# The last third of an MLP weight held behind another unit's keys, and a new hand-written order for the first batch

## The chip, the cores and the metric

The kernel runs on one core of one Trainium2 chip. The core has TensorE (PE; its weight loads are shown apart as PEld), VectorE (DVE), ScalarE (ACT), GpSimd (POOL) and SyncE (SP), which run side by side and wait for each other by semaphores. Each takes its own instructions in the order in which the program lists them. Transfers between HBM and on-chip memory are issued from the queues of SP, ACT and POOL and run on 16 shared DMA engines. The metric is device time in microseconds, the median of several executions; lower is better.

## The reference

Inputs are q, k and v of shape (8, 12, 448, 64): batches, heads, tokens, head width.

```python
def rmsnorm(x, g):
    rms = np.sqrt(np.mean(x * x, axis=-1, keepdims=True) + 1e-06)
    return x / rms * g
q_n, k_n = (rmsnorm(q, g_q), rmsnorm(k, g_k))
scores = scale * np.matmul(q_n, k_n.transpose(0, 1, 3, 2))
attn = softmax(scores)                                  # over the keys
x = np.matmul(attn, v) -> transposed to (8, 448, 768)
xn = (x - mean) / np.sqrt(var + 1e-06) * g_ln
out = x + np.maximum(xn @ w_ch1, 0.0) @ w_ch2           # 768 -> 3072 -> 768
```

## The kernel before

**Tiling.** Heads go in pairs: a batch has 6 pairs, and pair p = 6 * batch + number. The inputs come in units. Units 0 to 3 are the first batch; from unit 4 on a unit is two pairs (four heads), so batch 1 is units 4 to 6, batch 2 units 7 to 9, and unit 4 holds pairs 6 and 7, unit 5 pairs 8 and 9, unit 6 pairs 10 and 11. The keys, queries and values of a unit are each loaded by one DMA of 384 KB (tokens 0 to 383, `load_main`, line 169) and two of 32 KB (the 64 tokens left, `load_left`, line 177), from the SP queue for all units of the first 118 us but one DMA. Unit tiles from unit 5 on use two buffers in turn, so unit u + 2 can be loaded only when all readers of unit u are through.

**Weights.** The two MLP matrices are read in five pieces from GpSimd's queue: W0, W1 and W2 are the thirds of the first weight (`load_w1`, line 961, 1536 KB each as stored), W3 and W4 the halves of the second (`load_w2`, line 966, 2304 KB each). A piece that stands in `BEHIND` first copies two elements of a unit's tile into a scratch tile, `poke` (line 837), and so waits until that unit's load has landed; the number behind the unit is 0 for queries, 1 for keys, 2 for values. All that GpSimd has after it in the list waits too.

```python
BEHIND = {0: (4, 1), 2: (5, 2), 3: (6, 2), 4: (7, 2)}
def weights(c):
    if c in BEHIND:
        u, n = BEHIND[c]
        g = 6 * UNITS[u][2]
        nc.gpsimd.tensor_copy(out=poke, in_=self.loads[u][n][:, g - 1:g + 1, 0])
    if c < 3:
        self.load_w1(1024 * c, 1024 * c + 1024)
    else:
        self.load_w2(c - 3)
```

**Order.** The order of all instructions of the first stage is written out by hand in `ORDER`, a list of 580 short names; `first_attention` calls what each stands for, one after the other, on all five engines (tc.manual_schedule). The first stage covers the first batch's attention, layer norm and the up half of its MLP, the attention of the second batch, and most of the first batch's down half. Later work (`run_rest`) is laid out by a rule and is not touched. The names, with the engine that does each:

- `F12`: 12 filler matmuls of 128 columns on TensorE (line 877), whose result nobody reads.
- `L6k`, `L6q`, `L6v`: loads of a unit's keys, queries, values (SP). `W0` to `W4`: the weight pieces (POOL). `G` loads the norm's gains, `G2` scales them (POOL, line 885).
- For a unit u from 4 on: `a`, `c` square keys and queries, `d`, `e` sum the squares (DVE, line 265), `g` takes the inverse roots (ACT), `i` multiplies the keys by the gains (POOL, line 273), `j` makes their 16-bit copy, `k` the rest that this copy leaves (DVE, line 281), `l` scales the queries (DVE, line 93), `m` doubles them (line 318), `v`, `za`, `zb` copy the values (POOL, lines 321 and 327).
- For the first batch, in parts: `a`, `d`, `h`, `n`, `j`, `k` for the keys; `qa`, `qG` (times gains, line 604), `qt`, `ql` (scaled, line 611), `qm` (doubled, line 617), `Q0.0` to `Q2.4` (turned on TensorE) and `QC` (moved out of PSUM) for the queries; `z`, `za`, `zb` for the values (POOL, lines 660 and 665).
- `K8`, `Q8`: keys and queries of pair 8 turned on TensorE (lines 341 to 344, 358 to 361); all such turns write one PSUM tile, `tr`, which `C8`, `D8` empty (DVE, lines 351 and 366).
- `S`, `E`, `V`, `O`: scores (TensorE), their powers (ACT), times values (TensorE), divided by the sums (DVE). `T`, `A`, `N`, `X`, `XC`: layer norm and its turn. `U0.4`: a group of 24 matmuls of the up half (line 748), tile 0, columns 4 * 512 and on of the first weight, so U.0 and U.1 read W0, U.2 and U.3 W1, U.4 and U.5 W2; `R0.4` its relu. `H`, `J`, `P`: the down half (line 1088), which reads W3 for the first 384 columns and W4 for the others, its sum and its store. `Y.`: the second batch's layer norm, `Y.X` its turns by DMA.

`ENGINE` gives, for operations that several engines can do, the engine where it is not the usual one (A for ACT, V for DVE, P for POOL). Usual are ACT for `a`, `c`, `j` and `R`, POOL for `i` and `qG`, DVE for `n`, `m`, `qm`, `QC` and `C`.

Of the kernel before, what the change touches and what calls it, by code (L numbers as in the profile page):

```python
# [35 lines left out]
ORDER = """
F12 a0 d0 h0 sp1 a1 L4k G qa0.0 n0 spm sp2 L4q j0 qt0.0 d1 qG0.0 k0 F14 K0 h1 ql0.0 n1 a2 Q0.0
qa0.2 j1 C0 k1 d2 qt0.2 QC0.0 F2 K1 F10 S0.0.0 qa1.0 qG0.2 a3 qt1.0 qG1.0 d3 h2 S0.0.1 E0.0.1
E0.0.0 h3 C1 n2 n3 ql0.2 W0 j2 F36 S0.1.0 S0.1.1 k2 F9 Q0.2 K2 ql1.0 C2 W1 j3 E0.1.0 F5 Q1.0
E0.1.1 K3 QC0.2 S0.2.0 k3 z2 qa2.0 C3 S0.2.1 Q1.3 qt2.0 K4 C4 E0.2.0 E0.2.1 S0.3.0 qa2.4 z0 za2  # L40
S0.3.1 zb2 za0 QC1.0 zb0 hq E0.3.1 E0.3.0 z3 F6 K5 za3 S0.4.0 zb3 G2 S0.4.1 C5 QC1.3 V0.0
E0.4.0 qt2.4 qG2.0 E0.4.1 S0.5.0 S0.5.1 V0.1 E0.5.0 S1.0.0 V0.2 E0.5.1 L4v S1.0.1 V0.3 O0.0
E1.0.0 S1.1.0 E1.0.1 E1.1.0 V0.4 S1.1.1 E1.1.1 ql2.0 S1.2.0 S1.2.1 hr qm2.0 V0.5 V1.0 O0.1 V1.1
E1.2.1 S1.3.0 T0.1 T0.0 E1.2.0 E1.3.0 Q2.0 S1.3.1 b4 a4 V1.2 S1.4.0 qG2.4 E1.3.1 Q2.2 S1.4.1 A0
QC2.0 E1.4.0 N0 V1.3 S1.5.0 E1.4.1 S1.5.1 ql2.4 V1.4 E1.5.0 S2.0.0 O1.0 X0 E1.5.1 S2.0.1 E2.0.0
E2.0.1 V1.5 XC0 S2.0.2 L5k L5v E2.0.2 qm2.4 QC2.2 Q2.4 O1.1 d4 S2.1.0 c4 S2.1.1 U0.0 E2.1.1
E2.1.0 S2.1.2 S2.2.0 T1.1 T1.0 e4 E2.1.2 V2.0 A1 N1 S2.2.1 U0.1 E2.2.0 i4 S2.2.2 E2.2.1 j4 g4
l4 S2.3.0 m4 R0.0 E2.2.2 V2.1 S2.3.1 X1 E2.3.0 E2.3.1 QC2.4 S2.3.2 E2.3.2 XC1 V2.2 S2.4.0
E2.4.0 S2.4.1 L5q Q6 k4 D6 W2 V2.3 E2.4.1 R0.1 S2.4.2 O2.0 E2.4.2 S2.5.0 K6 E2.5.0 V2.4 S2.5.1
S2.5.2 C6 E2.5.2 T2.0 U1.0 R1.0 E2.5.1 b5 a5 c5 V2.5 O2.1 S6.0 E6.0 S6.1 K7 U1.1 S6.2 v4 E6.1  # L50
S6.3 E6.2 U1.2 E6.3 i5 za4 S6.4 T2.1 C7 A2 L6k d5 e5 v5 zb4 S6.5 U1.3 Q7 batch1 R1.1 N2 D7 j5
E6.4 L6v S6.6 k5 U0.2 E6.5 X2 R1.3 g5 l5 za5 S7.0 E6.6 V6.0 XC2 zb5 S7.1 V6.1 E7.0 L6q V6.2
V6.3 V6.4 W3 L7k V6.5 R0.2 E7.1 b6 a6 V6.6 S7.2 L7q K8 C8 O6 S7.3 m5 E7.3 E7.2 v6 i6 U0.3 L7v
za6 Q8 S7.4 V7.0 V7.1 S7.5 E7.4 E7.5 D8 V7.2 V7.3 U1.4 S7.6 S8.0 K9 d6 R1.2 c6 e6 E8.0 C9 zb6
j6 R0.3 U0.4 g6 U2.0 Q9 V7.4 k6 E7.6 V7.5 S8.1 S8.2 l6 L8k m6 R2.0 R0.4 E8.2 D9 U2.1 S8.3 V7.6
K10 b7 a7 i7 O7 U2.2 E8.3 R2.1 E8.1 S8.4 R2.2 S8.5 E8.4 L8v U2.3 V8.0 V8.1 E8.5 d7 S8.6 c7 U1.5
V8.2 j7 E8.6 R2.3 U0.5 E9.6 S9.0 C10 R0.5 V8.3 V8.4 V8.5 E9.0 S9.1 T7 V8.6 R1.4 U2.4 Q10 S9.2
e7 E9.1 O8 R1.5 k7 D10 v7 V9.0 S9.3 V9.1 E9.3 g7 l7 U2.5 Q11 S9.4 W4 E9.2 S9.5 E9.4 D11 E9.5
H0.0.0 S10.0 V9.2 za7 S10.1 E10.0 L8q K11 V9.3 b8 a8 V9.4 S10.2 V9.5 V9.6 E10.2 E10.1 H0.0.1
S10.3 m7 H0.0.2 E10.3 S10.4 S10.5 O9 R2.5 E10.4 V10.0 C11 zb7 E10.5 c8 R2.4 V10.1 V10.2 H0.0.3  # L60
Q12 v8 i8 L9k V10.3 S10.6 E10.6 H1.0.0 d8 S11.0 H1.0.1 T9 D12 j8 V10.4 e8 V10.5 E11.6 za8 V10.6
R S11.1 zb8 H1.0.2 O10 k8 E11.1 E11.0 K12 S11.2 H1.0.3 J0.0 S11.3 V11.0 g8 L9v L9q E11.2 V11.1
H2.0.0 S11.4 V11.2 E11.3 l8 C12 J1.0 S11.5 H2.0.1 E11.5 E11.4 K13 V11.3 S12.0 S12.1 m8 V11.4
V11.5 C13 V11.6 H2.0.2 E12.0 L10k O11 T11 S12.2 H2.0.3 H0.1.0 Y.A H0.1.1 E12.2 H0.1.2 Y.N2 Y.N0
S12.3 H0.1.3 x8 L10v L10q H1.1.0 Q13 E12.3 Y.X0 H1.1.1 S12.4 Y.R E12.4 J0.1 Y.N1 H1.1.2 H1.1.3
H2.1.0 S12.5 Y.X1 Y.X2 J2.0 E12.1 E12.5 H2.1.1 H2.1.2 D13 Y.N3 J1.1 Y.X3 H2.1.3 y8 J2.1 P2.1
P1.1 P0.1 P2.0 M
""".split()
# [1297 lines left out]
```

## Time and profile before

| | us |
|---|---|
| median of 3 runs | 596.11 |
| lowest and highest | 591.86, 599.5 |
| the profiled execution, its own time | 598.79 |
| its span in the profile | 597.1 |
| TensorE busy | 580.4 (97%) |
| DVE, ACT, POOL busy | 297.2, 346.6, 187.5 |
| the 94 filler matmuls, busy | 8.9 |
| last matmul group of the down half in the list (H2.1.3) begins | 117.2 |

A row of the order of time has start, duration, engine, line, operation, output <- inputs, and in brackets the engine's idle time before it with what ended it. A row of busy time by stretches has the stretch, its length, and for PE, PEld, DVE, ACT and POOL the busy time with the number of instructions, then the granted TensorE clock (1.00 is full), the DMA engines' share and the GB/s that they moved. A row of a DMA queue has packets, MB and the share of the 16 engines' time: q1 is SP's queue, q0 GpSimd's. A row of DMA issues has the transfer, the number of them, the size of one and the median time from issue to landing. A row of a group has its line and form, its number, then busy time and mean duration in ns, then idle time before it.

### The profile page before, as it was taken

Reading aid. Unit: us, or ns where it says so; the run is one execution under the profiler, and the core shown is the slowest. Engines: PE = TensorE matmul, PEld = TensorE weight load, DVE = VectorE, ACT = ScalarE, POOL = GpSimd, SP = SyncE. Lnnn points to the kernel's source line nnn. Section 1 sums busy time; section 2 is a strip of 40 time slices with the busy share of each in tenths; the row PEclk is TensorE's granted clock in tenths of the full one; section 3 lists DMA queues with packets and bytes.
Section 4 is the critical chain, followed back from the end, with each engine's and each line's share of the span. In section 5 each row is a group of like instructions: output and inputs, shape, how many; then the busy total and the mean of one; then the engine's idle time right before and its main releaser. Section 6 shows DMA issues by size and latency. Waiting matters only on the chain.

```text
span 597.1 us, 12428 instructions
## 1 busy us (share of the span) xinstructions
PE 580.4 (97%) x4974; PEld 362.5 (61%) x4974; DVE 297.2 (50%) x645; ACT 346.6 (58%) x654; POOL 187.5 (31%) x255
## 2 busy tenths in 40 slices
...
GB/s 258 211 241 218 196 211 205 148 113 144 153 142 141 105 133 137 177 135 88 153 108 115 140 105 149 192 121 126 133 56 90 86 63 1 27 106 1 1 53 56
DMA packets 130225, 75.24 MB, mean 126 GB/s; under 512 B 96469, under 2 KB 120357, under 8 KB 130165
## 3 DMA queue, kind: packets, MB, share of 16 engines
...
## 4 chain that ended last, share of the span: by engine, by line
PE 83%; DMA 7%; SPq 4%; DVE 4%; POOL 1%; issue 1%; POOLq 0%; DVEq 0%
PE psC L1088 35%; PE psH L1054 33%; PE psS L407 7%; DMA qkv<-in_v_dram 6%; PE oA L476 5%; SPq L177 2%; PE oB L478 2%; PE psS L425 1%; SPq L169 1%; DMA w<-in_k_dram 1%; DMA xnT<-xn 0%; DVE hT L758 0%; POOL v L660 0%; SPq L1036 0%; POOL vl L665 0%
## 5 line engine op out<-in xcount | busy, mean ns | idle before, releaser
L1088 PE MATMUL psC<-w,hT 128*128 128x384 f16 (+1 forms) x1368 | 235.6, 323 | 0.0
L1054 PE MATMUL psH<-xnT,w 128*128 128x512 f16 (+1 forms) x1008 | 217.3, 356 | 0.4 <-DMA xnT<-xn 0.4
L439 ACT ACTIVATE E<-psS,rr_all 128x448 f16<-128x448 f32 x264 | 164.5, 635 | 67.4 <-PE psS L407 66.8
L1088 PEld LDWEIGHTS <-hT 128*128 128x128 f16 x1368 | 128.2, 98 | 76.1 <-issue 0.4
L1056 ACT ACTIVATE hT<-psH 128x512 f16<-128x512 f32 (+1 forms) x168 | 93.7, 558 | 114.9 <-PE psH L1054 113.3
L1054 PEld LDWEIGHTS <-w 128*128 128x128 f16 x1008 | 91.1, 98 | 77.6 <-issue 2.9
L407 PE MATMUL psS<-qU,kU 128*128 128x448 f16 x252 | 86.7, 354 | 0.0
L476 PEld LDWEIGHTS <-E 128*128 128x128 f16 x792 | 53.9, 99 | 34.6 <-issue 2.5
L1095 DVE SCALAR_TENSOR_TENSOR x<-psC,rs_all,x 128x384 f32<-128x384 f32 x48 | 29.1, 616 | 77.9 <-PE psC L1088 77.4
L273 POOL TENSOR_TENSOR qkv<-qkv,gprod 128x896 f32<-128x896 f32 x19 | 39.5, 2079 | 76.6 <-ACT khl L118 62.1
L476 PE MATMUL oA<-v,E 128*128 128x65 f16 x756 | 57.8, 194 | 0.1
L489 DVE RECIPROCAL rec_all<-oA 128x6 f32<-128x6 f32 x42 | 8.2, 195 | 88.0 <-PE oA L476 87.7
L265 DVE TENSOR_REDUCE ssq<-khl 128x14 f32<-128x896 f32 x21 | 22.7, 1081 | 53.6 <-ACT khl L118 53.6
L169 POOL DMA_DIRECT2D qkv<-in_k_dram x14 | 11.1, 796 | 118.3 <-ACT E L439 53.4
L478 PE MATMUL oB<-v,E 128*128 128x65 f16 x252 | 45.1, 194 | 0.1
L407 PEld LDWEIGHTS <-kU 128*128 128x128 f16 x252 | 24.3, 98 | 15.2
L265 DVE TENSOR_REDUCE ssq<-qn 128x14 f32<-128x896 f32 x21 | 22.8, 1084 | 20.9 <-ACT qn L118 20.9
L93 DVE SCALAR_TENSOR_TENSOR qn<-qkv,rr_all 128x256 f16<-128x256 f32 (+2 forms) x71 | 25.2, 415 | 15.1 <-ACT rr_all L269 15.1
L748 PE MATMUL psU<-xnT,w 128*128 128x128 f16 x432 | 27.5, 222 | 0.0
L748 PEld LDWEIGHTS <-w 128*128 128x128 f16 x432 | 25.8, 100 | 1.6 <-issue 0.7
L478 PEld LDWEIGHTS <-E 128*128 128x128 f16 x264 | 25.6, 97 | 0.3 <-DVE xl L496 0.2
L491 DVE TENSOR_TENSOR x<-oA,rec_all 128x384 f32<-128x384 f32 x42 | 23.4, 558 | 1.3
(163 smaller groups left out, 599.5 us busy)
## 6 DMA issues: line engine op xcount, KB each, us to landing
out_dram<-x SPq DMA_DIRECT2D x20, 384.0 KB, 2.6
qkv<-in_v_dram POOLq DMA_DIRECT2D x15, 384.0 KB, 6.7
qkv<-in_k_dram POOLq DMA_DIRECT2D x14, 384.0 KB, 4.0
qkv<-in_q_dram POOLq DMA_DIRECT2D x14, 384.0 KB, 5.1
w<-in_moe_w_ch_dram POOLq DMA_DIRECT2D x3, 1536.0 KB, 14.5
...
qkv<-in_q_dram SPq DMA_DIRECT2D x7, 384.0 KB, 6.8
qkv<-in_v_dram SPq DMA_DIRECT2D x6, 384.0 KB, 12.9
```

Of the source, the lines that this page charges most:

```text
L93: nc.vector.scalar_tensor_tensor(out=out, in0=x, scalar=8.0, in1=r.unsqueeze(2).broadcast_to([x.shape[0], g, D]), op0=ALU.mult, op1=ALU.mult)
L265: nc.vector.tensor_reduce(out=c["ssq"][:, n], in_=c["sq", n], axis=AX.X, op=ALU.add)
L273: _on(nc, f"i{u}", "P").tensor_tensor(out=self.loads[u][1], in0=self.loads[u][1], in1=sh.gprod.unsqueeze(1).broadcast_to([128, g, D]), op= ...
L407: self.nc.tensor.matmul(ps[:, 0:S], c["main"][:, ts(i, 128)], c["q"][:, ts(i // 3, S)], start=True, stop=True)
L439: self.nc.scalar.activation(out=o, in_=c.pop(("ps", i))[:, 0:S], func=AFT.Exp, scale=self.units[u][3][:, g:g + 1], bias=EXP_BIAS)
L476: nc.tensor.matmul(oA[:, t, cs], E[:, ts(t, 128)], rhs, start=(i == 0 and t == 0), stop=(i == 6 and t == 2))
L478: nc.tensor.matmul(oB[:, cs], E[:, 320:448], rhs, start=(i == 0), stop=(i == 6))
L748: nc.tensor.matmul(ps[:, ts(f, 128)], sh.w1[:, dc, ts(4 * k + f, 128)], self.xnT[:, dc, ts(t, 128)], start=(f == 0 and dc == 0), stop=(f = ...
L1054: nc.tensor.matmul(ps[:, 0:N], sh.w1[:, dc, ts(f, 128)], xnT[:, dc, 0:N], start=(dc == 0), stop=(dc == NDC - 1))
L1056: nc.scalar.activation(out=hT[:, f, 0:N], in_=ps[:, 0:N], func=AFT.Relu)
L1088: nc.tensor.matmul(self.psC[:, 0:g[1]], self.hT[:, f, ts(t, 128)], sh.w2[:, h, f, c:c + g[1]], start=(f == 0), stop=(f == NFF - 1))
L1095: self.nc.vector.scalar_tensor_tensor(out=x, in0=self.sums.pop((b, t, g[0]))[:, 0:g[1]], scalar=self.rs[:, b, t:t + 1], in1=x, op0=ALU.mul ...
```

## The change

Three tables change, and no code.

- `BEHIND`: key 2 goes from (5, 2), unit 5's values, to (6, 1), unit 6's keys. Key 2 is W2, the last third of the first weight; W3, the first half of the second weight, keeps its hold on unit 6's values.
- `ENGINE`: from POOL to DVE n0; from DVE to POOL qG2.0, a7, i7; from POOL to ACT a4, j6, j7; from ACT to POOL a5, j5, c8; from DVE to POOL qm2.0, m7, m8; from ACT to DVE a1, QC2.2; from DVE to ACT QC0.0, QC2.4; from POOL to DVE qG1.0, c7; of the relus R0.0, R0.5 and R2.3 from ACT to DVE, R0.1, R0.4, R1.0, R1.2, R1.4, R1.5, R2.2, R2.4 and R2.5 from DVE to ACT.
- `ORDER`: the same names in another order; the fillers are 102 in place of 94.

```diff
-ENGINE = dict(x.split(":") for x in """ a0:V n0:P j1:P C1:A QC0.2:A qG2.0:V QC2.2:A qm2.4:P
-R0.1:V R0.2:V R0.4:V R1.0:V R1.2:V R1.4:V R1.5:V R2.0:V R2.2:V R2.4:V R2.5:V a4:P c4:P j4:P
-m4:P m5:P j6:P m6:P a7:V c7:P i7:V j7:P j8:P""".split())
+ENGINE = dict(x.split(":") for x in """ a0:V a1:V j1:P C1:A QC0.0:A QC0.2:A qG1.0:V qm2.0:P
+qm2.4:P QC2.4:A R0.0:V R0.2:V R0.5:V R2.0:V R2.3:V c4:P j4:P m4:P a5:P j5:P m5:P m6:P a7:P c7:V
+m7:P c8:P j8:P m8:P""".split())
...
-BEHIND = {0: (4, 1), 2: (5, 2), 3: (6, 2), 4: (7, 2)}
+BEHIND = {0: (4, 1), 2: (6, 1), 3: (6, 2), 4: (7, 2)}
```

Of `ORDER`, the names of the engines on which the prediction's steps lie, drawn out in their order before (-) and after (+). GpSimd from the first part's gains to unit 8:

```diff
-n0 qG0.0 j1 qG0.2 qG1.0 W0 W1 z2 z0 za2 zb2 za0 zb0 z3 za3 zb3 G2 a4 qG2.4 qm2.4 c4 i4 j4 m4
-W2 v4 i5 za4 v5 zb4 za5 zb5 W3 m5 v6 i6 za6 zb6 j6 m6 c7 j7 v7 W4 za7 zb7 v8 i8 j8 za8 zb8
+qG0.0 j1 qG0.2 z0 W0 W1 z2 za0 zb0 z3 za2 za3 zb3 zb2 G2 qG2.0 qm2.0 qG2.4 qm2.4 c4 i4 m4 j4
+v4 v5 za5 a5 W2 zb5 za4 i5 j5 zb4 W3 v6 za6 i6 m5 zb6 a7 m6 i7 W4 v7 za7 zb7 m7 v8 c8 i8 j8 za8
+zb8 m8
```

TensorE from pair 6's scores to the first reader of W2, ACT around c6, and DVE around ql2.0, around e6 and around k8 (the short minima that go with E6.6, E8.6 and E10.6 on DVE are left out):

```diff
 TensorE
-S6.0 S6.1 K7 U1.1 S6.2 S6.3 U1.2 S6.4 S6.5 U1.3 Q7 S6.6 U0.2 X2 S7.0 V6.0 S7.1 V6.1 V6.2 V6.3 V6.4
-V6.5 V6.6 S7.2 K8 S7.3 U0.3 Q8 S7.4 V7.0 V7.1 S7.5 V7.2 V7.3 U1.4
+S6.0 S6.1 K7 U1.2 S6.2 S6.3 U0.1 S6.4 Q7 S6.5 U0.2 S6.6 V6.0 S7.0 U0.3 S7.1 V6.1 V6.2 S7.2 X2 U1.3
+S7.3 V6.3 V6.4 K8 U2.0 S7.4 S7.5 V6.5 Q8 V6.6 U2.1 K9 S7.6 U0.4
 ACT
-g5 E6.6 E7.0 E7.1 a6 E7.3 E7.2 E7.4 E7.5 c6 E8.0 R0.3 g6
+R0.1 g5 a6 E6.6 E7.0 E7.1 R0.3 E7.2 E7.3 c6 j6 R1.3 E7.4 g6 R2.1 E7.5
 DVE
-qt2.4 qG2.0 O0.0 ql2.0 qm2.0 O0.1 T0.1 T0.0 A0 QC2.0 N0 ql2.4 O1.0 XC0
+d4 QC1.3 qt2.4 O0.0 ql2.0 O0.1 T0.0 T0.1 A0 QC2.0 ql2.4 N0 QC2.2 O1.0 O1.1 XC0
...
-D8 d6 R1.2 e6 C9 k6 l6
+C8 R0.2 e6 D8 k6 l6 R2.0 C9
...
-d8 T9 D12 e8 O10 k8 J0.0 l8 C12
+d8 e8 k8 D12 l8 C12 O10
```

More of the change, by code (lines that the diff above doesn't have):

```diff
@@ L36 @@
 ORDER = """
[L37 to L66, printed above, removed]
@@ L67 @@
-P1.1 P0.1 P2.0 M
+F12 L4k G a0 d0 h0 sp1 a1 n0 qa0.0 j0 spm sp2 qG0.0 d1 qt0.0 h1 k0 F13 K0 ql0.0 n1 Q0.0 C0 j1
+k1 a2 QC0.0 d2 qa0.2 qa1.0 qt0.2 qG0.2 z0 F2 K1 S0.0.0 a3 E0.0.0 h2 qt1.0 d3 S0.0.1 E0.0.1 C1
+n2 F44 S0.1.0 ql0.2 L4q Q0.2 j2 qG1.0 h3 E0.1.0 W0 k2 S0.1.1 F8 K2 W1 n3 C2 F14 K3 E0.1.1 qa2.0
+QC0.2 j3 ql1.0 S0.2.0 S0.2.1 Q1.0 z2 za0 zb0 z3 za2 E0.2.0 E0.2.1 za3 zb3 zb2 G2 C3 qG2.0
+S0.3.0 k3 S0.3.1 K4 QC1.0 Q1.3 E0.3.0 C4 L4v S0.4.0 E0.3.1 qt2.0 K5 C5 S0.4.1 b4 a4 qa2.4 V0.0
+E0.4.0 E0.4.1 hq F5 S0.5.0 E0.5.0 S0.5.1 V0.1 L5k E0.5.1 F4 S1.0.0 d4 E1.0.0 V0.2 S1.0.1 QC1.3
@@ new lines @@
+E1.0.1 qt2.4 V0.3 O0.0 S1.1.0 ql2.0 S1.1.1 V0.4 E1.1.0 S1.2.0 E1.1.1 V0.5 S1.2.1 E1.2.0 O0.1
+T0.0 E1.2.1 S1.3.0 V1.0 T0.1 S1.3.1 V1.1 E1.3.0 S1.4.0 qm2.0 Q2.0 qG2.4 A0 E1.3.1 hr QC2.0
+ql2.4 E1.4.0 S1.4.1 N0 Q2.2 L5v S1.5.0 V1.2 E1.4.1 S1.5.1 qm2.4 V1.3 E1.5.0 V1.4 S2.0.0 E1.5.1
+S2.0.1 E2.0.0 X0 V1.5 S2.0.2 E2.0.1 QC2.2 O1.0 S2.1.0 c4 E2.0.2 Q2.4 O1.1 E2.1.0 XC0 S2.1.1
+E2.1.1 QC2.4 V2.0 S2.1.2 e4 T1.0 S2.2.0 U0.0 T1.1 A1 E2.1.2 S2.2.1 E2.2.0 g4 E2.2.1 i4 N1 l4
+S2.2.2 m4 V2.1 L5q E2.2.2 S2.3.0 X1 j4 v4 S2.3.1 E2.3.0 V2.2 E2.3.1 S2.3.2 E2.3.2 S2.4.0 XC1
@@ new lines @@
+U1.0 E2.4.0 S2.4.1 S2.4.2 Q6 R0.0 E2.4.1 E2.4.2 V2.3 S2.5.0 v5 V2.4 S2.5.1 E2.5.0 R1.0 L6k k4
+D6 O2.0 za5 b5 a5 K6 S2.5.2 U1.1 E2.5.1 C6 T2.0 E2.5.2 V2.5 S6.0 S6.1 R1.1 O2.1 E6.0 E6.1 K7
+U1.2 c5 W2 S6.2 S6.3 d5 T2.1 C7 zb5 za4 i5 j5 U0.1 A2 zb4 R1.2 E6.3 S6.4 L6v E6.2 E6.4 Q7 S6.5
+E6.5 U0.2 S6.6 V6.0 L6q e5 D7 S7.0 N2 R0.1 g5 b6 a6 E6.6 W3 U0.3 l5 k5 v6 S7.1 V6.1 E7.0 za6
+E7.1 V6.2 S7.2 X2 i6 d6 XC2 R0.3 E7.2 U1.3 S7.3 V6.3 V6.4 m5 K8 C8 L7k batch1 R0.2 E7.3 U2.0
+S7.4 zb6 c6 S7.5 V6.5 Q8 e6 j6 V6.6 U2.1 R1.3 E7.4 g6 D8 L7q L7v k6 K9 S7.6 R2.1 E7.5 U0.4 E7.6
```

13 lines of the change are left out of this document (added).

## The prediction, made before any run of the change

> **What bounds the kernel now.** I read the page first, then busy time by stretches of time, then the chain of waits, and then the order of time on TensorE, GpSimd and the DMA queue around the one place where TensorE stands.
>
> ```profile
> span 597.1 us, 12428 instructions
> ```
>
> ```profile
> 30.00:35.00 5.00, 4.91 (x87) 4.49 (x85) 4.87 (x12) 4.86 (x10) 3.51 (x5) 1.00 1.12 228
> 55.00:60.00 5.00, 3.01 (x58) 2.65 (x56) 3.11 (x9) 2.87 (x5) 0.36 (x2) 1.00 1.10 280
> 60.00:65.00 5.00, 2.72 (x31) 2.28 (x32) 1.90 (x3) 1.38 (x3) 5.00 (x5) 0.75 0.91 170
> 65.00:70.00 5.00, 5.00 (x77) 4.73 (x76) 3.84 (x5) 2.72 (x6) 1.48 (x4) 0.91 1.24 212
> 300.00:400.00 100.00, 100.00 (x789) 61.26 (x788) 54.02 (x123) 57.82 (x112) 37.76 (x53) 1.00 0.73 134
> ```
>
> Each row gives length, then busy us of PE, weight loads, DVE, ACT, POOL, then the granted clock, the DMA share and GB/s. From 300 to 400 us TensorE is never idle, and the change reaches only about the first 118 us, so any time won or lost there passes to the end unchanged. From 30 to 35 us DVE (4.87 of 5) and ACT (4.86) are as full as TensorE. From 55 to 65 us TensorE loses 4.3 us, and the granted clock then falls to 0.75 and 0.91.
>
> ```profile
> 56.51 1.50 PE L748 MATMUL psU<-xnT,w 128*128 128x128 f16 x24
> 62.28 0.23 PE L358 MATMUL tr<-id,qn 128*128 128x128 f16 x1 [4.27 <-POOL qn L318]
> ```
>
> ```profile
> 45.28 0.19 POOL L837 COPY poke<-qkv 128x2 f32<-128x2 f32 x1 [3.86 <-DMA qkv<-in_v_dram]
> 45.74 0.91 POOL L961 DMA_DIRECT2D w<-in_moe_w_ch_dram  x1 [0.27 <-issue]
> 59.36 0.18 POOL L837 COPY poke<-qkv 128x2 f32<-128x2 f32 x1 [7.79 <-DMA qkv<-in_v_dram]
> 59.82 1.47 POOL L966 DMA_DIRECT2D w<-in_moe_w_ch_dram  x1 [0.27 <-issue]
> 61.28 0.94 POOL L318 COPY qn<-qn 128x896 f16<-128x896 f16 x1
> ```
>
> The first pair of GpSimd rows is W2, the second W3, the last m5. Q8 on TensorE wants m5; m5 is queued on GpSimd behind W3; W3 waits for unit 6's values (L6v).
>
> ```profile
> 29.15 15.68 DMA qkv<-in_v_dram
> 45.49 12.91 DMA qkv<-in_v_dram
> ```
>
> In the chain of waits L6v is the second row: issued at 45.49, landed at 58.40. It is slow because W2 was issued at 45.74 and shares the transfer engines with it. The next two fences split the traffic by queue: 50 to 55 us, with W2 in flight, and 43 to 46 us, with no weight.
>
> ```profile
> q0 software_dynamic: 402, 0.82, 86.6%
> q1 hardware_dynamic: 402, 0.31, 24.6%
> ```
>
> ```profile
> q1 hardware_dynamic: 1540, 0.87, 93.1%
> ```
>
> Beside W2 the unit loads (q1) get 0.31 MB in 5 us, 62 GB/s; alone 0.87 MB in 3 us, 290 GB/s.
>
> **The change, part by part.**
>
> *W2's new hold.* Key 2 is W2, the last third of the first weight. It now waits for unit 6's keys.
>
> ```profile
> qkv<-in_k_dram SPq DMA_DIRECT2D x1, 384.0 KB, 6.0
> qkv<-in_k_dram SPq DMA_DIRECT2D x2, 32.0 KB, 3.9
> ```
>
> ```profile
> qkv<-in_v_dram SPq DMA_DIRECT2D x1, 384.0 KB, 12.9
> qkv<-in_q_dram SPq DMA_DIRECT2D x1, 384.0 KB, 11.6
> ```
>
> ```profile
> 41.42 1.17 SPq L169 DMA_DIRECT2D qkv<-in_k_dram  x1
> 45.49 1.46 SPq L169 DMA_DIRECT2D qkv<-in_v_dram  x1
> 48.43 0.59 SPq L169 DMA_DIRECT2D qkv<-in_q_dram  x1
> ```
>
> L6k lands at 41.42 + 6.0 = 47.4, its left rows a little later, so W2's poke passes near 47.8 in place of 45.28: 2.5 us later. In 2.5 us the unit queue alone moves 0.72 MB; L6v is 384 + 64 KB, 0.46 MB. So L6v should land near 51 to 52, not 58.4, and part of L6q with it. What is queued behind W2's wait on GpSimd: zb5, za4, i5, j5, zb4, W3, v6, za6, i6, m5.
>
> ```profile
> L273 POOL TENSOR_TENSOR qkv<-qkv,gprod x19: 2074/2077/2088, 47.4 to 451.6; 128x896 f32<-128x896 f32 x19
> ```
>
> ```profile
> L321 POOL CAST v<-qkv 128x768 f16<-128x768 f32 x20 | 16.5, 825 | 21.8 <-PE oB L478 21.8
> L327 POOL CAST vl<-qkv 64x128 f16<-64x128 f32 x40 | 11.6, 291 | 6.6 <-PE oB L478 5.4
> ```
>
> From 47.8: W2 with its gap 1.4, zb5 and za4 0.6, i5 2.1, j5 0.9, zb4 0.3 give 53.1 (i5 by the first of these rows, v and z pieces by the others, j5 like m5, 0.94). L6v is there, so W3 runs at once, 1.9: 55.0; v6 0.8, za6 0.3, i6 2.1, m5 0.9: m5 ends at 59.1. TensorE came to Q8 at 62.28 - 4.27 = 58.0. The new list has one more U group before Q8 (nine, not eight; one is at most the 1.50 of the row above, some 1.35 pipelined), so it comes there at 59.4 or later. The 4.27 goes, and with it the clock loss, 5 x 0.25 + 5 x 0.09 = 1.7.
>
> ```profile
> w<-in_moe_w_ch_dram POOLq DMA_DIRECT2D x1, 1536.0 KB, 13.1
> ```
>
> W2 took 13.1 us from issue to landing, so it should land near 61.3. Its first reader, U0.4, stands behind Q8, U2.1 and K9, near 62.5 or later, so this costs nothing; without that cover 1 us.
>
> *What is late next.* L6q now starts under W2 with some 0.2 to 0.35 MB left, at 62 GB/s: 3 to 6 us from 51, more for its small left rows, so 58.5 to 60.8. ACT's list is E7.2, E7.3, c6, j6, R1.3, E7.4, and c6 reads L6q.
>
> ```profile
> 56.71 1.16 ACT L439 ACTIVATE E<-psS,rr_all 128x448 f16<-128x448 f32 x2
> 64.79 0.94 ACT L118 ACTIVATE qn<-qkv 128x896 f32<-128x896 f32 x1
> ```
>
> E7.3 and E7.2 ended at 57.9; with one U group more ahead of S7.3, ACT comes to c6 near 59. Behind c6 wait e6 and D8 on DVE (so K9, which needs D8's bank) and E7.4 (so S7.6). I take 0.8; bounds 0 and 2.5.
>
> *The engine moves.* DVE's work up to the end of the first batch's attention is the same within 0.3 us: n0, a1, qG1.0, QC2.2 and R0.0 come, qG2.0, qm2.0, QC0.0, QC2.4, R0.1 and R1.0 go. One move meets its reader: qG2.0 goes to GpSimd, behind G2, and ql2.0 on DVE waits for it.
>
> ```profile
> 26.94 2.14 POOL L885 TENSOR_SCALAR gln<-gln 128x768 f32<-128x768 f32 x1
> 30.80 1.13 POOL L604 TENSOR_TENSOR qkv<-qkv,gprod 128x256 f32<-128x256 f32 x2
> ```
>
> ```profile
> 25.29 1.39 DVE L604 TENSOR_TENSOR qkv<-qkv,gprod 128x512 f32<-128x512 f32 x2
> 27.38 1.27 DVE L611 TENSOR_TENSOR qn<-qkv,rr_all 128x512 f16<-128x512 f32 x2
> ```
>
> G2 starts 0.8 earlier (z0 is now ahead of W0) and ends at 28.3; qG2.0, twice qG2.4's 1.13 us, at 30.5. ql2.0 stood at 27.38, so DVE idles 2 to 3 us where it is nearly full; qm2.0, now on GpSimd, holds Q2.0 too. Against that DVE drops 2.0 us (qG2.0, qm2.0) near that place, and ACT carries a4 and QC0.0 (+1.3 in sum up to E2.0.0), itself at 4.86 of 5. I put TensorE 1.5 us later at the end of this stage; bounds 0 and 3. Eight fillers more at 53 ns, 0.4 us, lie in these waits and count nothing; without that cover 0.4.
>
> The later swaps (R's, a5, j5, a7, c7, j7, m7 and others) lie where DVE has room, 3.84 of 5 in the row from 65; I count nothing, but c8 is a rival below. The stores and turns at the list's end change order only: 0.
>
> GpSimd's share of the work grows, and here the Trainium skill speaks against the change: "SBUF — State Buffer", section "Who interferes with whom", has a DVE instruction with two inputs in SBUF and a GpSimd instruction that reads SBUF block each other for a whole instruction. The row of L273 above does not agree: 19 such GpSimd instructions took 2074 to 2088 ns while DVE was half busy.
>
> *Sum*, against the profiled execution's own 598.79 (span 597.1 and 1.7 around it): 598.79 - 4.27 - 1.7 + 0.8 + 1.5 = 595.1, 3.7 less. That execution lay 2.7 above the median of 596.11, so against the median the same terms give 592.4. The waits vary from run to run; I keep 595.
>
> The Trainium skill, "TensorE: Matmul & The Clock Gate", "What's actually happening", has the clock halve after an idle window of about 3.4 us that runs free. By that a wait of 4.27 us need not always cost the 1.7, and a run without it would be at 597.1. The trace's clock rows show one such drop only.
>
> **The rivals.**
>
> *A longer wait at K12 (slower).* c8 moves from ACT to GpSimd, between v8 and i8, and k8 now stands before D12 on DVE.
>
> ```profile
> 33.88 1.68 POOL L120 TENSOR_TENSOR qn<-w 128x896 f32<-128x896 f32 x1
> ```
>
> ```profile
> 94.52 0.60 DVE L366 COPY qU<-tr 128x896 f16<-128x896 f16 x1
> ```
>
> ```profile
> 97.53 0.22 PE L341 MATMUL tr<-id,khl 128*128 128x128 f16 x1
> ```
>
> The chain is: L8q landed, c8 1.7 (c4's row, the same square on GpSimd), i8 2.1, j8 0.9, k8 1.1, D12 0.6, then K12: 6.4 and hand-overs. K12 stood at 97.5 and would stand near 94; so it decides if L8q lands after about 87.5. W3 now follows W2 and W4 follows W3 almost without a pause, and beside W3 the units get less:
>
> ```profile
> q0 software_dynamic: 613, 0.47, 79.2%
> q1 hardware_dynamic: 573, 0.39, 41.6%
> ```
>
> That is 64 to 68 us: 98 GB/s, 14 us for a unit of 1.38 MB. L7 from 60 to 74, L8 to 88 or 90, then K12 waits 2 to 4 us and the clock drops: 595 + 4 + 1.7 = 601. For it: this arithmetic. Against: W4 waits for L7v, and in a pause of 2 us L8 gains 4. Chance 0.20.
>
> *The hold doesn't do what it says.* L6v still isn't through when W2 runs. W3's poke then stays near 59.4, and m5 has v6, za6 and i6 ahead of it now: 59.4 + 1.9 + 0.8 + 0.3 + 2.1 + 0.9 = 65.4 against TensorE at 60.9: 4.5 and the clock's 1.7 on 594.3 give 600.5. Against: 0.72 MB fit where 0.46 are wanted. Chance 0.12.
>
> *GpSimd and DVE block each other*, as a mechanism of this kernel: i5, j5, v6, i6 and m5 each behind a DVE instruction of 1.1 make m5 3.5 to 4 late at Q8: 599. That is the page's rule from above; chance 0.04.
>
> *Better.* DVE fills its idle time and L6q is there for c6: neither 1.5 nor 0.8, so 592.8, and against the median 590. Chance 0.12.
>
> **How the numbers follow.** My forecast has 0.52, its own range 591 to 599. To leave out no more than 2 in 10, the range goes from 589 to 603. Two per cent is 11.9 us, about what a measurement tells from no change. Faster than 584.2 is more than all the terms together: 0.02. Slower than 608 takes both slow rivals in one run and the early bound: 0.07. The rest, 0.91, lies within.
>
> **What would show it.** Right: Q8 without a GpSimd wait; clock 1.00 from 60 to 70; W2's poke near 47.8 and W3's soon after 53 without a DMA wait; ACT idle before c6; DVE idle before ql2.0, released by GpSimd. Wrong: a DMA wait at W3's poke, TensorE idle at K12 behind D12, TensorE more than 3 us late at the end of the first batch's attention, or a unit's load that lands so late that another engine stands before it.

## The result, and the profile after

| | before | after |
|---|---|---|
| median, 22 runs each | 593.57 us | 597.72 us |
| lowest and highest | 591.25, 599.5 | 596.25, 601.03 |
| the profiled execution (span) | 598.79 (597.1) | 599.01 (597.4) |

The ratio is 1.0063, with a 95% interval from 1.0039 to 1.0086: the change costs 0.4 to 0.9%, where a gain of some 0.6% on the profiled execution was forecast. The two profiled executions are alike only because the first one of the kernel before lay 5.2 us above its median of 22.

The place that the forecast was about came out as foretold. These are GpSimd's rows in the changed kernel, W2 and its hold, W3 and its hold, and m5:

```profile
48.79 0.19 POOL L837 COPY poke<-qkv 128x2 f32<-128x2 f32 x1 [0.55 <-DMA qkv<-in_k_dram]
49.25 0.91 POOL L961 DMA_DIRECT2D w<-in_moe_w_ch_dram  x1 [0.28 <-issue]
...
54.92 0.92 POOL L837 COPY poke<-qkv 128x2 f32<-128x2 f32 x1
55.79 1.47 POOL L966 DMA_DIRECT2D w<-in_moe_w_ch_dram  x1
...
60.30 0.93 POOL L318 COPY qn<-qn 128x896 f16<-128x896 f16 x1
```

The hold waits 0.55 us, W3's hold no longer waits for a transfer, and m5 is done at 61.2. L6v, issued at 46.08 in this execution, took 4.1 us to land and no longer 12.9:

```profile
qkv<-in_v_dram SPq DMA_DIRECT2D x1, 384.0 KB, 4.1
```

TensorE runs through Q8 without a wait, and the clock holds. What was won is lost further on; these are the rows of busy time by stretches:

```profile
55.00:60.00 5.00, 5.00 (x93) 4.73 (x91) 3.83 (x5) 4.20 (x8) 5.00 (x5) 1.00 1.12 201
60.00:65.00 5.00, 4.94 (x82) 4.45 (x79) 4.78 (x7) 4.11 (x9) 1.53 (x3) 1.00 1.22 229
...
110.00:115.00 5.00, 4.02 (x25) 2.18 (x23) 1.14 (x3) 0.63 (x1) 0.00 (x0) 1.00 0.83 183
115.00:120.00 5.00, 2.35 (x6) 0.87 (x7) 0.28 (x3) 0.00 (x0) 0.00 (x0) 0.70 0.69 157
```

From 55 to 65 us TensorE is busy 9.94 us in place of 5.73. From 110 to 120 it is busy 6.37 of 10, and the clock drops to 0.70. The order of time on TensorE names the wait. It stands behind H2.1.3, the last group of the down half in the list, at the first group of the second batch's up half (line 1054); the expectations below, which say before or at H2.1.3, mean this one:

```profile
117.66 3.68 PE L1054 MATMUL psH<-xnT,w 128*128 128x512 f16 x10 [3.64 <-DMA xnT<-xn]
```

In the kernel before the same row had a wait of 0.41:

```profile
118.70 1.67 PE L1054 MATMUL psH<-xnT,w 128*128 128x512 f16 x7 [0.41 <-DMA xnT<-xn]
```

So TensorE came there 4.3 us earlier (117.66 - 3.64 against 118.70 - 0.41) and left 1.0 us earlier. The lower clock took the rest: the first thirty matmuls behind the wait took 8.00 us, in the kernel before 6.63, and the scores behind them start at 125.49 against 125.17. TensorE waits for the second batch's turned layer norm, Y.X0 to Y.X3, which are DMAs from SP's queue. SP's rows of the changed kernel (x8, L10k, left rows of L10v, L10q, and then the four turns):

```profile
93.91 7.37 SPq L297 DMA_TRANSPOSE kU<-khl  x1
101.33 2.50 SPq L300 DMA_TRANSPOSE kU<-khl  x2
103.94 0.52 SPq L169 DMA_DIRECT2D qkv<-in_k_dram  x1
104.50 1.30 SPq L177 DMA_DIRECT2D qkv<-in_k_dram  x2
105.84 2.14 SPq L177 DMA_DIRECT2D qkv<-in_v_dram  x2
108.96 0.38 SPq L169 DMA_DIRECT2D qkv<-in_q_dram  x1
109.38 1.26 SPq L177 DMA_DIRECT2D qkv<-in_q_dram  x2
110.75 5.23 SPq L1036 DMA_TRANSPOSE xnT<-xn  x4
```

In the kernel before that last row reads:

```profile
111.80 5.23 SPq L1036 DMA_TRANSPOSE xnT<-xn  x4
```

The queue is a second floor that didn't come down with what TensorE won: the turns leave 1.05 us earlier than in this execution, and TensorE comes 4.3 earlier. Beside a second profile of the kernel before (c1_before, at 594.61, further down), which has no wait at Q8, they even leave 2.85 us later:

```profile
107.90 5.23 SPq L1036 DMA_TRANSPOSE xnT<-xn  x4
```

That was the first theory after the result (theory 1 in the expectations). It is only a part.

### The profile page after: what moved, and what is told of

It reads as the page before. It is cut to its first block, busy times and chain, and to the rows that moved or that the text cites. A ratio compares the mean times of both kernels' runs of the same rounds, so it can differ in the third digit from the quotient of the medians.

```text
span 597.4 us, 12434 instructions
## 1 busy us (share of the span) xinstructions
PE 580.9 (97%) x4982; PEld 361.5 (61%) x4982; DVE 292.3 (49%) x635; ACT 349.0 (58%) x660; POOL 195.4 (33%) x259
## 4 chain that ended last, share of the span: by engine, by line
PE 86%; DMA 8%; SPq 3%; POOL 2%; DVE 1%; issue 0%; ACT 0%; POOLq 0%
PE psC L1088 34%; PE psH L1054 33%; PE psS L407 7%; PE oA L476 4%; DMA w<-in_moe_w_ch_dram 4%; DMA qkv<-in_v_dram 2%; PE psU L748 2%; PE oB L478 2%; PE psS L425 1%; DMA qkv<-in_k_dram 1%; SPq L169 1%; SPq L177 1%; PE psS L692 1%; PE oA L724 0%; DMA xnT<-xn 0%
## 5 line engine op out<-in xcount | busy, mean ns | idle before, releaser
L273 POOL TENSOR_TENSOR qkv<-qkv,gprod 128x896 f32<-128x896 f32 x20 | 41.6, 2079 | 83.3 <-ACT khl L118 68.8
```

Source lines behind the costliest of these rows:

```text
L273: _on(nc, f"i{u}", "P").tensor_tensor(out=self.loads[u][1], in0=self.loads[u][1], in1=sh.gprod.unsqueeze(1).broadcast_to([128, g, D]), op= ...
```

## The experiments

Ratios are to the kernel before, timed on the same chip beside each run, with 95% intervals. Line numbers in the experiments' rows lie up to three lower than above, where their lists of names have fewer lines.

| run | what it is | median us | ratio |
|---|---|---|---|
| e1_hold_in_old | old list, new hold, W2 behind zb4 | 597.59 | 1.0084 [1.0045, 1.0122] |
| e2_list_alone | new list, old hold | 596.24 | 1.0065 [1.0042, 1.0089] |
| e3_turns_first | changed, turns ahead of L10v, L10q | 597.38 | 1.0060 [1.0032, 1.0089] |
| e5_no_block | changed, GpSimd pauses behind W3 | 594.77 | 1.0026 [0.9999, 1.0054] |
| e6_no_block_turns_first | both | 594.03 | 1.0011 [0.9987, 1.0034] |
| e7_old_early | old early part, changed rest | 597.90 | 1.0070 [1.0045, 1.0094] |
| e8_new_early | new early part, old rest | 593.46 | 0.9994 [0.9972, 1.0015] |
| e9_old_early_both_moves | old early part, rest of e6 | 593.52 | 0.9993 [0.9968, 1.0018] |
| e12_hold_old_place | old list, new hold alone | 594.31 | 1.0024 [1.0001, 1.0047] |
| e10_w2_behind_v4 | old list, W2 behind v4 | 593.37 | 0.9989 [0.9962, 1.0016] |
| e13_block_in_old | old list, v6, za6, i6 ahead of m5 | 596.89 | 1.0023 [0.9987, 1.0059] |
| e14_old_turns_first | old list, turns first | 591.91 | 0.9971 [0.9938, 1.0004] |
| e16_old_turns_first_again | the same | 592.00 | 0.9970 [0.9934, 1.0007] |
| e15_new_early_turns_first | new early part, rest of e14 | 593.53 | 1.0002 [0.9976, 1.0028] |

Single profiled executions: the kernel before 594.61 (c1_before); the changed kernel 596.48, 598.86, 597.81 (c2_after, c3_after, c4_after).

### The turns first in the changed kernel

SP's queue, in its order from L10k:

```diff
-L10k L10v L10q Y.X0 Y.X1 Y.X2 Y.X3 P2.0 y8
+L10k Y.X0 Y.X1 Y.X2 Y.X3 L10v L10q P2.0 y8
```

> The changed kernel with one move: the loads of unit 10's values and queries (L10v, L10q), which nobody wants before the third batch, stand behind Y.X3 on SP's queue. Theory 1 (SP's queue at the end of the list is the floor): the turns Y.X leave SP's queue at 105 to 107 in place of 110.75, the last lands at 112 to 114, the 3.64 us of TensorE at H2.1.3 and the half clock behind it go, and the time falls by 3 to 5 us against the changed kernel, to 593 to 595 (ratio to before 0.998 to 1.002). Theory 2 (the time is lost before, in the early stage or to later weights) and any theory that has the end of the list covered: no change, ratio 1.005 to 1.008.

The wait behind H2.1.3 went, and the median hardly moved. Its lowest time, 593.23, is 3 us below that of the changed kernel, but 7 of 11 executions lie above 596. The profiled one (599.59) shows why: TensorE stands in another place, at K8, where the changed kernel's first profile has no wait:

```profile
61.90 0.27 PE L339 MATMUL tr<-id,khl 128*128 128x128 f16 x1 [2.64 <-DVE xnT L782]
```

K8 waits for XC2, a DVE copy, and XC2 is late because of l5, three instructions ahead of it on DVE. DVE's rows in this kernel, l5 and k5:

```profile
54.88 4.50 DVE L91 SCALAR_TENSOR_TENSOR qn<-qkv,rr_all 128x896 f16<-128x896 f32 x1
59.30 1.08 DVE L279 TENSOR_TENSOR khl<-qkv,khl 128x896 f16<-128x896 f32 x1
```

An instruction of 1.08 us takes 4.50. GpSimd's rows at the same time, W3, v6, za6, i6 and m5:

```profile
53.84 1.47 POOL L964 DMA_DIRECT2D w<-in_moe_w_ch_dram  x1
55.31 0.84 POOL L319 CAST v<-qkv 128x768 f16<-128x768 f32 x1
56.07 0.30 POOL L325 CAST vl<-qkv 64x128 f16<-64x128 f32 x1
56.33 2.09 POOL L271 TENSOR_TENSOR qkv<-qkv,gprod 128x896 f32<-128x896 f32 x1
59.45 1.73 POOL L316 COPY qn<-qn 128x896 f16<-128x896 f16 x1 [1.02 <-DVE qn L91]
```

From W3 to i6 GpSimd works without a pause, and l5 ends one l5 (1.0 us) after i6 does. As soon as GpSimd has to wait for l5 itself, DVE goes on. So a second theory (called theory 4 in the expectations): GpSimd, fed without a pause, keeps a DVE instruction with two SBUF inputs waiting for 3 us.

### The hold alone, the list alone

```diff
-BEHIND = {0: (4, 1), 2: (6, 1), 3: (6, 2), 4: (7, 2)}
+BEHIND = {0: (4, 1), 2: (5, 2), 3: (6, 2), 4: (7, 2)}
```

> The new list and engines with W2's old hold (unit 5's values). Theory 1 (second floor at the end of the list): L6v lands near 58 again and TensorE waits some 4 us at Q8, but then comes later to H2.1.3 and waits less there for xnT; the time stays within 0.3% of the changed kernel's (ratio to before 1.003 to 1.010). Theory 2 (the hold costs): near the kernel before, ratio 1.002 or less. Theory 3 (the hold gains and the list loses): slower than the changed kernel by about 4 us, ratio 1.012 or more.

The new list is as slow with the old hold as with the new one, and W2 leaves at 47.40 in place of 49.25: in the new list the order on GpSimd, and not the hold, puts W2 behind L6v (issued at 44.39, landed after 4.3 us). None of the three theories had foreseen that. The profile shows the block again, with k5 at 4.10 us and 2.86 us of TensorE at K8:

```profile
56.01 4.10 DVE L281 TENSOR_TENSOR khl<-qkv,khl 128x896 f16<-128x896 f32 x1
```

In the old list, with W2 moved from behind D6 to behind zb4, so that L6k is listed ahead of it:

```diff
-D6 W2 V2.3
+D6 V2.3
...
-v5 zb4 S6.5
+v5 zb4 W2 S6.5
-BEHIND = {0: (4, 1), 2: (5, 2), 3: (6, 2), 4: (7, 2)}
+BEHIND = {0: (4, 1), 2: (6, 1), 3: (6, 2), 4: (7, 2)}
```

> The old list and engines; only W2's hold is the new one (unit 6's keys), and W2 stands behind zb4, since L6k has to be issued first. Theory 1 (the end of the list is a second floor: the layer-norm turns Y.X0 to Y.X3 leave SP's queue only at about 112 and the last lands near 118, whatever TensorE won before): the wait of TensorE at Q8 goes, L6v lands near 51, a wait of 2 to 4 us for xnT appears before H2.1.3, and the time stays within 0.3% of the kernel before (ratio 0.997 to 1.003). Theory 2 (the new hold itself costs, because W2, W3, W4 and the loads behind them all come later): slower than before, ratio 1.005 or more. Theory 3 (the hold is worth what was forecast and the new list takes it away): ratio 0.990 to 0.995.

It is slower by 0.84%, but not by the hold: W2 leaves only at 51.15, behind i5, and U1.4, W2's first reader in the old list, waits for it:

```profile
62.99 1.18 PE L746 MATMUL psU<-xnT,w 128*128 128x128 f16 x18 [2.68 <-DMA w<-in_moe_w_ch_dram]
```

Its place was badly chosen. At W2's old place, with L6k listed just ahead of it, the hold stands alone:

```diff
-D6 W2 V2.3
+D6 L6k W2 V2.3
-BEHIND = {0: (4, 1), 2: (5, 2), 3: (6, 2), 4: (7, 2)}
+BEHIND = {0: (4, 1), 2: (6, 1), 3: (6, 2), 4: (7, 2)}
```

> The kernel before with the new hold alone, at W2's old place in the list; L6k is listed just ahead of it, which changes nothing on SP's queue. Theory 5 (the wait at Q8 that the forecast wanted to remove stands in few executions of the kernel before; in most L6v leaves early enough and there is nothing to win, while W2 comes 2 to 3 us later and its first reader U1.4 waits for it): no wait at Q8, W2 lands at 60 to 62, TensorE waits 0 to 2 us at U1.4; ratio 0.999 to 1.005. Forecast's theory (4 to 6 us are won at Q8 in the typical execution): ratio 0.989 to 0.994.

1.0024, at the edge of what can be told. Q8 has no wait, and GpSimd stands for 6.55 us at the hold:

```profile
48.13 0.19 POOL L835 COPY poke<-qkv 128x2 f32<-128x2 f32 x1 [6.55 <-DMA qkv<-in_k_dram]
```

That stand has a price of its own: i5 comes later behind it, ACT waits 1.98 us for i5's result, and TensorE 1.55 us for ACT:

```profile
53.95 0.35 PE L419 MATMUL psS<-qU,kU 128*128 128x448 f16 x1 [1.55 <-ACT E L437]
```

At this place the hold alone wins nothing. Without these 1.55 us the ratio would be near 0.9998, an estimate from one profile, and still far from the 0.989 to 0.994 of the forecast's theory.

### A second profile of the kernel before

> The kernel before, unchanged, for a second profile. Theory 1 needs an execution near 592 to differ from the one profiled first (598.79) at Q8: a wait well under 4.27 us there, the clock near 1.00 from 60 to 70, and TensorE at H2.1.3 waiting for xnT or just not. If an execution near 592 shows the same wait at Q8, the spread lies elsewhere.

This execution, at 594.61, has Q8 at 60.39 without a wait, L6v landed 4.5 us after its issue, and full clock from 55 to 70 us. Its row of DMA issues for L6v, and of the order of time for Q8:

```profile
qkv<-in_v_dram SPq DMA_DIRECT2D x1, 384.0 KB, 4.5
```

```profile
60.39 0.22 PE L358 MATMUL tr<-id,qn 128*128 128x128 f16 x1
```

What the forecast meant to remove isn't there. Its clock fell at another place, from 25 to 30 us, behind a wait of 1.32 us for the first batch's values on GpSimd:

```profile
26.24 0.22 PE L724 MATMUL oA<-vl,E 128*128 128x130 f16 x1 [1.32 <-POOL vl L665]
```

```profile
25.00:30.00 5.00, 3.76 (x50) 3.75 (x50) 2.96 (x7) 2.36 (x6) 4.69 (x8) 0.66 1.12 211
```

In all, 148 executions of the kernel before were timed, 22 for the result and 126 beside the runs. Two of them, of 1554.7 and 1936.05 us, are left out here; the median of the other 146 is 593.4, and 31 of them are above 596. Of six profiles of kernels with this stretch as it was (the first, this one, e8, e14, e15, e16) two show the wait: the first, and e16, at 598.79 too:

```profile
62.64 0.29 PE L356 MATMUL tr<-id,qn 128*128 128x128 f16 x1 [4.30 <-POOL qn L316]
```

There L6v took 10.5 us, and the clock fell to 0.58 and 0.74, twice the loss of the first profile. Why L6v sometimes takes 10 to 13 us was tried with W2 one step later on GpSimd:

```diff
-D6 W2 V2.3
+D6 V2.3
...
-S6.2 v4 E6.1
+S6.2 v4 W2 E6.1
```

> The kernel before with W2 one step later on GpSimd, behind v4 (0.84 us), with the old hold. Theory 5: when L6v is issued only 0.25 us ahead of W2, as in the first profile of the kernel before, it lands 12.9 us later, and when it is issued 0.9 us ahead it lands after 4.6 us; one step behind, W2 never overtakes it, so L6v lands before 52, no execution has the long wait at Q8, and the median stays at the fast executions of the kernel before: ratio 0.996 to 1.000, spread under 4 us. If the spread of the kernel before has another source: as wide as before, ratio 0.999 to 1.002.

Inconclusive. The spread stayed as wide (590.8 to 600.3), and W2 didn't come later against L6v: v4 ran in GpSimd's wait, and W2 was issued 0.26 us behind L6v, as in the first profile, with L6v landed after 4.2 us all the same. In e8 and e15 it was issued 0.23 and 0.25 us behind, and L6v landed after 3.7 and 4.4. That lead does not decide. In the two profiles with the long transfer the issue itself took longer, 1.46 and 1.20 us against 0.60 in e8, e10, e14 and e15, but also 1.21 in the one at 594.61. L6k's issue just before was longer in these two as well, 1.17 and 1.07 us against 0.37 to 0.54 in the other five; nothing was tried on that. The cause stays open.

### Without the block

Behind W3 on GpSimd, m5 goes first, and what nobody needs yet stands behind a7, which waits for unit 7's keys; i6 goes to DVE, j6 stands later on ACT:

```diff
 GpSimd
-W3 v6 za6 i6 m5 zb6 a7 m6 i7 W4
+W3 m5 a7 v6 za6 zb6 m6 i7 W4
 DVE
-C8 R0.2
+C8 i6 R0.2
 ACT
-c6 j6 R1.3 E7.4
+c6 R1.3 E7.4 j6
```

> The changed kernel without GpSimd's unbroken work behind W3: i6 goes to DVE behind C8, j6 behind E7.4 on ACT, and v6, za6, zb6 behind a7 on GpSimd, where they are still early enough. Theory 4 (GpSimd, which the new hold has made work without a pause from W2 on, keeps a two-input DVE instruction, l5 or k5, waiting for 3 us or more, so that TensorE waits 2.6 to 2.9 us at K8): l5 and k5 take 1.1 to 2 us each, no wait at K8; the time falls by 1.5 to 3.5 us against the changed kernel, ratio to before 1.000 to 1.004, with what is left at the list's end (xnT) as a wait of up to 4 us in some executions. Rival (the blocked instruction is hidden, the time is lost in the early stage alone): no change, ratio 1.005 to 1.009.

1.0026 in place of 1.0063, by intervals that overlap, and l5 and k5 take 1.08 us each:

```profile
54.80 1.08 DVE L91 SCALAR_TENSOR_TENSOR qn<-qkv,rr_all 128x896 f16<-128x896 f32 x1
55.80 1.08 DVE L279 TENSOR_TENSOR khl<-qkv,khl 128x896 f16<-128x896 f32 x1
```

TensorE has no wait at K8 and waits 1.99 us behind H2.1.3. Then both moves, this one and that of e3_turns_first:

> Both: no unbroken GpSimd work behind W3, and the loads L10v and L10q behind Y.X3 on SP's queue. Theory 4 with theory 1 (two floors, of which each hides the other): neither a wait at K8 nor one at H2.1.3, 3 to 5 us under the changed kernel, ratio to before 0.997 to 1.002. If the early stage alone holds the loss: no change, ratio 1.005 to 1.009.

1.0011: 0.52% under the changed kernel, 3.1 us of its 3.7 (0.63% of 593.6), and here the two intervals do not meet. Eleven of its twelve executions lie below 595.3. The last wait, behind H2.1.3, is 0.22 us; SP issues the turns as soon as the layer norm has them:

```profile
108.18 5.22 SPq L1034 DMA_TRANSPOSE xnT<-xn  x4
```

Alone the turns won 0.03%, alone the block 0.37%, together 0.52%. The first two are within the noise. That each floor hides a part of the other fits the waits in the profiles; how much, these numbers don't tell.

### Which of the two the changed kernel meets

> The changed kernel as it is, for a second profile. Theory 4: in this one l5 or k5 takes 3 us or more between 54 and 60 us and TensorE waits at K8; if not, TensorE waits for xnT at H2.1.3 as in the first profile. If neither wait is there and the time is still near 597, the loss lies elsewhere.

> The changed kernel as it is, third look. The two-floor theory: either k5 or l5 takes 3 us or more and TensorE waits at K8, with little or no wait for xnT at H2.1.3, or neither is blocked and TensorE waits 2 to 4 us at H2.1.3. An execution with neither would be near 593.

> The changed kernel as it is, fourth look. As for the third: one of the two waits, not neither.

All four profiles of the changed kernel show the wait behind H2.1.3: 3.64, 2.28, 2.45 and 2.71 us. The turns leave SP's queue at 109.05 to 110.75 in them, and at 105.55 to 107.90 in three profiles with the old end of the list and no wait at Q8 (c1_before, e8, e10). One, the third, has the block as well. DVE's row of l5, and GpSimd's v6, za6 and i6:

```profile
54.08 3.92 DVE L93 SCALAR_TENSOR_TENSOR qn<-qkv,rr_all 128x896 f16<-128x896 f32 x1
```

```profile
53.83 0.93 POOL L321 CAST v<-qkv 128x768 f16<-128x768 f32 x1
54.71 0.28 POOL L327 CAST vl<-qkv 64x128 f16<-64x128 f32 x1
54.97 2.08 POOL L273 TENSOR_TENSOR qkv<-qkv,gprod 128x896 f32<-128x896 f32 x1
```

It cost 2.29 us at K8 in that execution, and the turns 2.45 more. In the other three l5 ran in 1.10 us, and zb4 and W3's copy on GpSimd are the ones lengthened, to 0.91 to 0.99 and 0.92 us where 0.29 and 0.19 are usual. So the late turns were paid in all four, the block in one. The expectation of one or the other was wrong.

That GpSimd's order alone makes the block was tried in the old list:

```diff
-W3 m5 v6 i6 za6
+W3 v6 za6 i6 m5
```

> The kernel before with one move: v6, za6 and i6 stand ahead of m5 on GpSimd, as in the new list. Theory 4: behind W3 GpSimd then doesn't pause for l5; k5 or l5 on DVE takes 2.5 us or more in place of 1.08, TensorE waits 1 to 3 us at K8 or Q8, ratio to before 1.002 to 1.007. If the block needs the rest of the new list: k5 and l5 at 1.08, ratio 0.998 to 1.002.

No block: in the old list k5 and l5 stand ahead of the others on DVE and were done before v6 began. So the order on GpSimd alone is not enough. But m5, behind 3.0 us of work that nobody waits for, held Q8:

```profile
60.78 0.23 PE L356 MATMUL tr<-id,qn 128*128 128x128 f16 x1 [2.79 <-POOL qn L316]
```

The median lies 0.5% above the one beside it (596.89 against 593.95), but the ratio is 1.0023 and its interval holds 1: a loss is likely, not shown.

### The early part

The lists and engines are joined at the first scores of pair 2: here the old one up to there, and what is left in the new order.

```diff
-F12 L4k G a0 d0 h0 sp1 a1 n0 qa0.0 j0
...
+F12 a0 d0 h0 sp1 a1 L4k G qa0.0 n0
...
 L5k d4 L5v qm2.4 S2.0.0 E1.5.1
```

> The kernel before up to the first scores of pair 2 (its order and its engines), and from there the changed kernel with its new hold. Early-stage theory (1.5 us or more are lost before 50 us because qG2.0 and the rest of the new order hold TensorE up): ratio to before 1.000 to 1.004. Theory 4 alone (the loss is made between 50 and 62 us): no better than the changed kernel, ratio 1.005 to 1.009, with l5 or k5 blocked for 3 us or more.

No better than the changed kernel: k5 then meets GpSimd in full, 5.39 us in the profiled execution, and K8 waits 3.52.

```profile
54.67 5.39 DVE L278 TENSOR_TENSOR khl<-qkv,khl 128x896 f16<-128x896 f32 x1
```

The other way round, the new early part and the old rest with the old hold:

```diff
-F12 a0 d0 h0 sp1 a1 L4k G qa0.0 n0
...
+F12 L4k G a0 d0 h0 sp1 a1 n0 qa0.0 j0
...
 S2.0.0 O1.0
```

> The changed kernel up to the first scores of pair 2 (order and engines), and from there the kernel before with its old hold. It has neither the new hold nor GpSimd's unbroken work behind W3. Early-stage theory: TensorE is 1.5 us later at 50 us, most of it before turned queries (Q2.0, which waits for qm2.0 on GpSimd); nothing behind it takes that back or adds to it, so ratio to before 1.001 to 1.005. If the early stage costs nothing in the end: 0.998 to 1.001. If it alone is the whole loss: 1.005 to 1.009.

0.9994: no loss that can be measured. Then the old early part with both moves, that is e7's list with the edits of e5 and e3:

> Old early part (to the first scores of pair 2), then the changed kernel with its new hold and with both moves: no unbroken GpSimd work behind W3 (i6 to DVE, v6, za6, zb6 and j6 later), L10v and L10q behind Y.X3. The three terms found (blocked DVE instruction, late turns, early stage) are all gone. Theory: 1 to 2.5 us under the kernel with both moves and the new early part (ratio 1.001), so ratio to before 0.994 to 0.999. If the early part isn't worth anything: 0.999 to 1.003.

0.9993, 0.18% or 1.1 us under e6, with intervals that overlap. Its profile still has a wait of 1.37 us behind H2.1.3.

### The turns first in the kernel before

```diff
-x8 L10v L10q Y.X0 Y.X1 Y.X2 Y.X3 y8
+x8 Y.X0 Y.X1 Y.X2 Y.X3 L10v L10q y8
```

> The kernel before with L10v and L10q behind Y.X3 on SP's queue. In its profiles TensorE waits 0.4 to 0.5 us for xnT at H2.1.3; that is all there is to win: ratio 0.997 to 1.001. If the late turns hold it up as they do the changed kernel: 0.993 to 0.996.

> The kernel before with L10v and L10q behind Y.X3, measured a second time. If its gain is real: ratio to before 0.995 to 0.999, lowest times under 591. If the first measurement was chance: 0.999 to 1.002.

0.9971 and 0.9970: medians 1.5 to 2 us under the kernel before beside them, lowest times (590.63 and 590.77) some 0.5 us under. That is more than the wait of 0.4 to 0.5 us that was expected to go; the rest is not explained. Each interval ends just above 1 (1.0004, 1.0007). Two measurements that agree make the gain likely; neither shows it alone. TensorE is then never idle from 100 to 120 us:

```profile
100.00:110.00 10.00, 10.00 (x67) 6.12 (x66) 5.54 (x8) 2.73 (x6) 0.00 (x0) 1.00 0.55 109
110.00:115.00 5.00, 5.00 (x27) 2.45 (x25) 0.90 (x3) 1.19 (x2) 0.00 (x0) 1.00 0.62 151
115.00:120.00 5.00, 5.00 (x32) 2.40 (x30) 1.93 (x2) 4.23 (x7) 2.11 (x2) 1.00 0.21 44
```

It has the lowest median and ratio of all versions tried. With the new early part in front of it (e8's front, this rest):

> The changed kernel up to the first scores of pair 2, then the kernel before with its old hold and with L10v and L10q behind Y.X3. If the new early part costs the 1 us or more that its later Q2.0 suggests: 0.6 to 2 us slower than the same without it, ratio to before 0.998 to 1.001. If it costs nothing: 0.995 to 0.998.

1.0002, a median of 593.53 against 592.00 of the old early part beside it on the same chip: with the end of the list free, the new early part costs about 1.5 us, by medians whose intervals overlap.

## Why the forecast was wrong

**The step that gave it the wrong sign: 4.27 and 1.7 as a gain of the typical execution.** Both numbers stand in the first profile, and e16 repeats the wait (4.30 us) with twice the clock loss. But they belong to executions of 598.79, and 115 of 146 executions of the kernel before are at 596 or less; the profile at 594.61 has no wait at Q8 and full clock there. The forecast set 598.79 beside a median of three runs, 596.11, wrote that "the waits vary from run to run", and kept 595. Against the typical 593.4 the same sum without these two terms would have been 593.4 + 0.8 + 1.5 = 595.7: slower. The hold alone (e12), at 1.0024, bears it out.

The size of the clock's loss, 1.7, was right where the wait stands: from Q8 to K9 TensorE needed 4.79 us in the first profile and 3.17 in the second, 1.6 more. The reason given for the wait was not enough: the forecast put L6v's 12.9 us down to W2, issued 0.25 us behind it, but with W2 as close behind, L6v landed after 3.7 to 4.4 us in e8, e10 and e15. What makes it slow in some executions stays open.

That 597.72 lies within 589 to 603 is luck: in the typical execution the two gains of the sum are missing, and two losses that it left out stand in their place.

**The step that missed the rest: "The stores and turns at the list's end change order only: 0."** In the new list x8 stands ahead of L10k, and L10v and L10q stand ahead of the turns as before; the turns left at 110.75, 3 us after the last layer norm's instruction on DVE, and in all four profiles 1.1 us or more later than in c1_before. How much of that is x8's place was not tried. TensorE waited 2.3 to 3.6 us for them in all four profiles, and in three of the four the clock dropped after it. Order in a queue is a time, as soon as the engine that reads its result comes earlier.

**The rival given 0.04, GpSimd and DVE blocking each other, is the third part.** The forecast turned it down because i6's kind on GpSimd took 2074 to 2088 ns while DVE was half busy. That looked at the engine that goes first, not at the one that waits. The victim is DVE, where l5 or k5 took 3.92 to 5.39 us in four profiles with the later part of the new list (the third of the changed kernel, e2, e3, e7), by 2.8 to 4.3 us more than 1.08. The Trainium skill, "SBUF — State Buffer", section "Who interferes with whom", was right: a DVE instruction with two SBUF inputs and a GpSimd instruction that reads SBUF exclude each other. The rival had GpSimd behind DVE; where TensorE waited, it was the other way round. With block and turns both out, 3.1 of the 3.7 us went (e6); how much of it each has in a typical execution isn't settled, since each covers the other.

**The early part, 1.5 with bounds 0 and 3:** within its bounds, but not settled. e8 shows no loss, and its interval ends at 0.9 us; e9 against e6 gives 1.1 and e15 against e16 1.5, both by intervals that overlap. The place was off: ql2.0 waited 0.48 us for GpSimd in the first profile, not 2 to 3, since DVE's other work came in between; what is seen instead, in two of the four profiles, is TensorE at Q2.0, which waits for qm2.0 on GpSimd. The row of the second profile of the changed kernel:

```profile
32.48 0.51 PE L636 MATMUL psQ<-id,qn 128*128 128x128 f16 x6 [0.61 <-POOL qn L617]
```

**c6's wait, 0.8 with bounds 0 and 2.5:** 0. L6q left at 48.49, ahead of W2 at 49.25, and took 3.7 us; ACT's row of c6 has no wait:

```profile
59.33 0.94 ACT L118 ACTIVATE qn<-qkv 128x896 f32<-128x896 f32 x1
```

**Right:** L6v's landing (50.2 for 51 to 52), W2's landing near 62.4 ahead of its reader, Q8 without a wait and clock 1.00 from 60 to 70. m5's end came out 2.1 late (61.2 for 59.1): W2's hold passed 1.0 later, and DVE lengthened zb4 and W3's copy. The rival of K12 did not come: c8, which waits for L8q, began at 86.72, before the 87.5 that was named as its point, and K12 ran without a wait. Nor did the one in which the hold doesn't do what it says. The fillers and the later swaps of engines were not measured apart.
